# Sharing the float64-to-float32 conversion of the weights anew between VectorE, ScalarE and GpSimd, with a new written order of the opening and a later second half of batch 1's attention

## The chip, the cores and the metric

The kernel runs on one core of a Trainium2 chip. The metric is the device time of one execution in microseconds (us). The core has five engines with a queue of their own each: TensorE (PE, matrix products, with its weight loads PEld), VectorE (DVE), ScalarE (ACT), GpSimd (POOL) and SyncE (SP, which here only issues DMAs). Each takes its instructions in order.

## The reference, cut to what matters

Eight batches of 576 tokens with 8 heads of 64 attend to a memory of 32 slots per head, which is itself a weighted sum over the tokens. The result goes through a feed-forward layer with h * cos(h).

```
a    = softmax(phi over the 32 slots)                  # per token
k_m  = einsum(a, k);  v_m = einsum(a, v)               # 32 slots of 64 per head
attn = softmax(q @ k_m^T / 8)                          # over the 32 slots
x    = (attn @ v_m)  ->  4608 x 512
h    = x @ w_in                                        # 512 x 2048
out  = (h * cos(h)) @ w_out                            # 2048 x 512
```

`w_in` and `w_out` are float64 arrays (8 MB each); the others are float32.

## The kernel before, in words

**The fold.** x is never formed. Per batch, v_m is multiplied into w_in (the *fold*, `fold_psum`, L481), so h is a product of the attention weights (kept transposed in `aT`) and of the folded weights `vw`.

**Groups and steps.** The 4608 tokens are worked in twelve groups of 384. A step is one of 16 slices (128 wide) of the 2048 hidden columns of one group. It has a first product (`gemm1`, L548: into `hp`), h * cos(h) on ScalarE and VectorE (`act`, `act_end`), and a second product (`gemm2`, L600: into three accumulators), which runs four steps later (LAG). Group 0 uses float32 operands. The later groups use operands that are split into two float16 halves, three products for each. For this the weights must be scaled and split (`w_in_split`, L218; `w_out_split`, L209), with a scale that needs the largest sum of squares over all blocks of a weight (`m_of`, `s_of`).

**The opening.** Everything up to and with group 0's steps is written as single named steps, whose order is the string `ORDER` (L48). The instructions of a step go to the queues of their engines in that order, so an engine waits at the instruction whose turn it is. Names that matter here: `d_...` is a DMA issue on SP's queue (`d_kv0_c` the five pieces of batch 0's k and v, `d_q0_0` and `d_q0_1` its q, `d_in3` block 3 of w_in, `d_b1` batch 1's phi, k and v, `d_q1`, `d_q2` the later q); `warm*n` is n products of zeros; `ga` gathers the memory; `X`, `tpx`, `km`, `vm` turn it; `sc`, `tu`, `mx`, `sh`, `ex`, `to`, `no`, `ba`, `sp`, `sq` are scores, turn, maximum, shift, exp, total, normalise, turn back, high half and low half of the attention; `ffj` folds block j for batch 0 and `vfj` keeps the result; `g1_f` is gemm1 of group 0, `a1_f` to `a4_f` its activation (ScalarE, VectorE, ScalarE, VectorE), `g2_f` its gemm2; `fo1`, `hi0`, `hi1` fold and split for the loop; `m_`, `mt_`, `s_` are the scales.

**The conversion.** The chip has no float64 arithmetic, so each block of a weight (16 blocks of 1 MB, in0 to in7 and out0 to out7) is turned into float32 by bits (`conversion`, L154), over 1024 elements in each of 128 partitions:

- *scale*: the high word, taken as float32, times 2^-112, in place (GpSimd, L172)
- *low*: the top byte of the low word becomes the three lowest bits, as int16 (ScalarE for 13 blocks, L169; VectorE for 3, L171)
- *sign*: the top byte of the high word becomes the sign bit, as int16 (GpSimd for 13 blocks, VectorE for in0, in4 and out2; both L164)
- *join*: the scaled word shifted left by 3, or the two halves (VectorE, L176)
- *square*: the sum of squares of the block, for the scale (ScalarE, L179)

Three buffers take the loads in turn (in2 and in3 go to parts of `wo`), so a load waits for the join of the block that had its buffer before it.

**The loop.** Behind the opening, `for i in range(NF, 12 * NF)` (L983) writes steps 16 to 191; step 16 to 31 are group 1, which holds the last 192 tokens of batch 0 and the first 192 of batch 1. With them are written the splits of the weights (one of w_out and one of w_in in each step of group 1), the folds, and the memory and attention of later batches in small pieces. The order of the loop's instructions on each engine is set by a planner, which may also let them slip in between those of the opening's end.

Of the kernel before, what the change touches and what calls it, by code (L numbers as in the profile page):

```python
# [55 lines left out]
a2_4 square_out0 low_in4 vf3 a3_4 low_out1 max1 a1_5 g2_1 a4_4 square_in3 low_in6 g1_6 top1 join_in4 ff4 scale_out1
a1_6 d_b1 a2_5 a3_5 sign_in6 sign_out1 square_in4 d_in5 join_out1 a2_6 vf4 g1_7 a1_7 join_in6 a4_5 a3_6 d_out2 a2_7
g2_2 square_in1 blank1 a3_7 be1_0 be1_1 a4_6 a4_7 scale_in5 square_in6 low_in5 sign_in5 ex0_2 scale_out2 g1_8 d_out3
d_q1 to0_2 no0_2 g2_3 ba0_2 join_in5 x1_1 x1_0 g1_9 ga1_0 ga1_1 low_out2 sign_out2 join_out2 square_out1 ga1_2 a1_8
ga1_3 scale_out3 ff5 ga1_4 den1 X1_0 a1_9 a2_9 g2_4 sign_out3 low_out3 vf5 X1_1 sp0_2 a2_8 a3_9 d_in7 tpx1 scale_in7  # L60
# [1009 lines left out]
```

## Time and profile before

| | |
|---|---|
| median of 3 runs | 723.73 us (723.27 to 724.03) |
| the profiled execution | 723.56 us, of which the span of the profile is 721.8 |
| granted TensorE clock, mean | 0.99 |
| DMA moved | 66.17 MB |

The page gives one profiled execution. Its busy times are shares of the span. Its 40 slices show, per engine, in which part of the span it worked; one slice is 18 us. A row of a timeline is: start, duration, engine, source line, operation, what it writes and reads, shape and type, count and, in square brackets, the idle time before it with what ended it. A row of a group is the same without times: busy us, mean ns of one, and the idle time before them with its releasers. A row by stretch has: from and to, length, then busy us (and instructions) of PE, PEld, DVE, ACT and POOL, the granted clock, the DMA share and GB/s.

### The profile page before, as it was taken

How to read it: one execution, taken by the hardware profiler on the slowest of the kernel's cores; microseconds unless marked ns; L12 is line 12 of the kernel's file. 1: busy time of each engine (PE TensorE's matmuls, PEld its weight loads, DVE VectorE, ACT ScalarE, POOL GpSimd, SP SyncE). 2: the span in 40 equal slices, each digit the busy share in tenths (PEclk: the TensorE clock that was granted, in tenths of full speed). 3: DMA queues.
4: the chain of work that ended last, by engine and by line, in shares of the span. 5: the costliest groups of instructions: out<-in, count | busy, mean ns of one | idle time of the engine just before them, and what ended most of it. 6: DMA issues, size and time to landing. Idle time of an engine off the chain costs nothing.

```text
span 721.8 us, 11827 instructions
## 1 busy us (share of the span) xinstructions
PE 695.8 (96%) x4582; PEld 356.7 (49%) x4582; DVE 537.4 (74%) x1119; ACT 512.6 (71%) x946; POOL 89.8 (12%) x59
## 2 busy tenths in 40 slices
PE   7778988999999999999999999999999999999997
PEld 3334434555454444565444444565444444555553
DVE  3877989999897986579776886579776896576552
ACT  2658886899787686678767696678767786665652
POOL 0898880000000000000000100000000000000000
PEclk9989999999999999999999999999999999999999
DMA  8967792143625300152103220152100010100101
GB/s 299 341 250 264 249 321 59 51 106 75 199 67 165 111 1 1 45 165 67 45 1 111 72 94 1 45 166 66 45 2 1 1 45 1 45 1 1 45 0 45
DMA packets 31480, 66.17 MB, mean 92 GB/s; under 512 B 2176, under 2 KB 11456, under 8 KB 31424
## 3 DMA queue, kind: packets, MB, share of 16 engines
q1 hardware_dynamic: 27104, 57.55, 24.6%
q10 hardware_dynamic: 4320, 7.87, 2.8%
q8 instruction: 36, 0.59, 0.4%
q14 instruction: 20, 0.16, 0.1%
HBM read 51.77 MB, written 9.44 MB: 85 GB/s over the span
## 4 chain that ended last, share of the span: by engine, by line
PE 77%; DVE 7%; POOL 6%; DMA 4%; issue 3%; ACT 2%; SPq 1%; POOLq 0%; DVEq 0%; ACTq 0%
PE acc L613 43%; PE hp L562 23%; PE pv L492 3%; POOL wo L164 3%; PE acc L608 3%; PE psA L253 2%; DMA raw_in<-in_w_in 2%; POOL w_in_sb L164 2%; PE sc L395 1%; DMA phi<-in_phi 1%; POOL raw_out L172 1%; DVE u L583 1%; PE pv L486 1%; DVE wo L176 1%; DVE u L592 1%
## 5 line engine op out<-in xcount | busy, mean ns | idle before, releaser
L613 PE MATMUL acc<-wo,gp 128*128 128x512 f16 x1584 | 371.5, 379 | 0.0
L613 PEld LDWEIGHTS <-gp 128*128 128x128 f16 x1584 | 153.3, 98 | 161.5 <-issue 2.9
L562 PE MATMUL hp<-aT,vw 128*128 128x192 f16 (+1 forms) x1440 | 202.4, 284 | 0.5 <-DVE u L592 0.5
L562 PEld LDWEIGHTS <-vw 128*128 128x128 f16 x1440 | 125.3, 98 | 80.8 <-issue 28.3
L588 ACT ACTIVATE u<-u,quarter 128x384 f32<-128x384 f32 x176 | 107.0, 614 | 69.9 <-DVE u L583 69.3
L592 DVE SCALAR_TENSOR_TENSOR u<-hp,u 128x384 f32<-128x384 f32 x176 | 96.7, 554 | 63.1 <-ACT u L588 62.4
L583 DVE SCALAR_TENSOR_TENSOR u<-hp,cu,gp 128x192 f32<-128x192 f32 (+1 forms) x240 | 115.3, 504 | 27.8 <-ACT gp L578 26.5
L578 ACT ACTIVATE gp<-hp,cu 128x192 int32<-128x192 f32 (+1 forms) x240 | 110.7, 490 | 24.7 <-PE hp L562 17.3
L595 DVE TENSOR_TENSOR gp<-u,gp 128x384 f16<-128x384 f32 x176 | 96.4, 552 | 33.8 <-ACT gp L594 33.5
L594 ACT CAST gp<-u 128x384 f16<-128x384 f32 x176 | 88.2, 508 | 42.2 <-DVE u L592 41.7
L608 PE MATMUL acc<-wo,gp 128*128 128x512 f32 x96 | 48.0, 639 | 5.1 <-DVE wo L176 5.1
L333 POOL PARTITION_ALL_REDUCE l<-l x6 | 2.6, 441 | 305.2 <-DVE l L279 305.2
L501 DVE SCALAR_TENSOR_TENSOR vw<-pv,vw 128x512 f16<-128x512 f32 x48 | 33.0, 689 | 6.8 <-ACT vw L499 6.4
L499 ACT ACTIVATE vw<-pv 128x512 f16<-128x512 f32 x48 | 28.4, 592 | 7.7 <-PE pv L492 7.3
L608 PEld LDWEIGHTS acc<-wo,gp 128*128 128x128 f32 x96 | 18.9, 207 | 28.3 <-issue 20.0
L164 POOL TENSOR_SCALAR wo<-raw_out 128x1024 int16<-128x1024 int8 x7 | 30.9, 4420 | 0.5
L553 PE MATMUL hp<-aT,vf 128*128 128x384 f32 x64 | 26.9, 548 | 3.3 <-DVE gp L883 2.9
L629 ACT ACTIVATE ob<-acc,os 128x512 f32<-128x512 f32 x28 | 18.5, 684 | 15.3 <-PE acc L613 12.1
L253 PE MATMUL psA<-kv,phi 128*32 128x129 f32 (+3 forms) x640 | 23.3, 276 | 1.2 <-DMA kv<-in_kv_first 1.2
L588 ACT ACT_TABLE_LOAD x17 | 21.8, 1283 | 0.3
L253 PEld LDWEIGHTS psA<-kv,phi 128*32 128x32 f32 (+1 forms) x640 | 16.2, 109 | 11.4 <-issue 7.1
L395 PE MATMUL sc<-q,km 128*64 128x256 f32 (+3 forms) x192 | 19.9, 336 | 0.1
(159 smaller groups left out, 602.2 us busy)
## 6 DMA issues: line engine op xcount, KB each, us to landing
kv<-in_kv SPq DMA_DIRECT2D x28, 516.0 KB, 5.7
raw_out<-in_w_out SPq DMA_DIRECT2D x8, 1024.0 KB, 5.0
q<-in_qT SPq DMA_DIRECT2D x7, 1152.0 KB, 6.2
out<-ob ACTq DMA_DIRECT2D x30, 256.0 KB, 2.1
raw_in<-in_w_in SPq DMA_DIRECT2D x6, 1024.0 KB, 9.2
phi<-in_phi SPq DMA_DIRECT2D x7, 512.0 KB, 5.2
w_in_sb<-w_in_parts SPq DMA_DIRECT2D x12, 256.0 KB, 4.5
phiT<-in_phiT SPq DMA_DIRECT2D x4, 576.0 KB, 5.0
```

Of the source, the lines that this page charges most:

```text
L164: engine.tensor_scalar(out=halves[:, :, :, 1], in0=high_top, scalar1=0.0, scalar2=-32768.0, op0=ALU.is_lt, op1=ALU.mult)
L253: nc.tensor.matmul(psA[32 * j:32 * (j + 1), g * KV:g * KV + wide], lhsT=a[:n, c, h * M:(h + 1) * M], rhs=kvs[c][:n, h * wide:(h + 1) * wid ...
L501: nc.vector.scalar_tensor_tensor(out=vw[:, 1, g], in0=src, scalar=T, in1=vw[:, 0, g], op0=ALU.mult, op1=ALU.subtract)
L562: nc.tensor.matmul(hp[:, c0:c0 + n], lhsT=vw[:, wi, g, fo * P:(fo + 1) * P], rhs=aT[:, ai, g, c1:c1 + n], start=(k == 0), stop=(k == 5))
L578: ins = nc.scalar.activation(ni[:, c0:c0 + n], hp[:, c0:c0 + n], AF.Copy, scale=turns, bias=0.25)
L583: nc.vector.scalar_tensor_tensor(out=u[:, c0:c0 + n], in0=hp[:, c0:c0 + n], scalar=turns, in1=ni[:, c0:c0 + n], op0=ALU.mult, op1=ALU.subt ...
L588: nc.scalar.activation(u, u, AF.Sin, scale=TWO_PI_BELOW, bias=quarter)
L592: nc.vector.scalar_tensor_tensor(out=u, in0=hp[:, :GT], scalar=2.0 ** -17, in1=u, op0=ALU.mult, op1=ALU.mult)
L594: nc.scalar.copy(gp[:, 0], u)
L595: nc.vector.tensor_tensor(out=gp[:, 1], in0=u, in1=gp[:, 0], op=ALU.subtract)
L608: nc.tensor.matmul(accs[grp][t], lhsT=gp[:, t * P:(t + 1) * P], rhs=wo[:, f + 1], start=(f == 0), stop=(f == NF - 1))
L613: nc.tensor.matmul(accs[grp][t], lhsT=gp[:, gi, t * P:(t + 1) * P], rhs=parts[:, wi], start=(f == 0 and gi == 0 and wi == 0), stop=(f == N ...
```

## The change

- All sixteen sign passes are done by VectorE.
- The low passes: ScalarE keeps eight (in0, in2, in6, in7, out2, out3, out6, out7), GpSimd gets five (in3, in4, out1, out4, out5), VectorE has three (in1, in5, out0).
- The scaling of eight blocks (in1, in2, in3, in4, in6, in7, out0, out5) goes to ScalarE; GpSimd keeps eight.
- vm1's two copies go from VectorE to ScalarE.
- The written order of the opening is another, with 75 warm products in place of 50, and with d_in0 ahead of the kv loads and d_in1 ahead of d_q0_0.
- Batch 1's attention for tokens 256 to 575 (blocks 1 and 2 of its three) leaves the opening. It is written in pieces into steps 18 to 25 of the loop, and d_q2 with it. The maximum and scale of w_out (m_out, mt_out, s_out, os_0) move into step 17.
- The splits of w_out are written two steps later, those of w_in in every second step of groups 1 and 2 in place of every step of group 1.

```diff
-LOW_ACT = set('in0 in1 in2 in3 in6 in7 out1 out2 out3 out4 out5 out6 out7'.split())
-SIGN_DVE = set('in0 in4 out2'.split())
+LOW_ACT = set('in0 in2 in6 in7 out2 out3 out6 out7'.split())
+LOW_POOL = set('in3 in4 out1 out4 out5'.split())
+SCALE_ACT = set('in1 in2 in3 in4 in6 in7 out0 out5'.split())
+COPY_ACT = set('vm1'.split())
...
-d_phiT0 d_eye d_kv0_0 max0 d_kv0_1 d_kv0_2 e0_1 e0_0 blank0 warm*15 w0_0 d_kv0_3 w0_1 k0_0 warm*1 ga0_0 ga0_1 den0
-d_kv0_4 k0_1 d_q0_0 w0_2 d_in0 d_in1 k0_2 ga0_2 ga0_3 ga0_4 X0_0 scale_in0 X0_1 warm*4 tpx0 km0 att0 low_in0 vm0
-bound0 warm*3 sc0_0 tu0_0 sc0_1 tu0_1 mx0_0 sign_in0 sh0_0 ex0_0 join_in0 to0_0 no0_0 scale_in1 d_q0_1 ba0_1_0
-ba0_0_0 d_in2 square_in0 low_in1 warm*20 ff0 ba0_1_1 vf0 d_out0 ba0_0_1 d_in3 sc0_2 warm*7 g1_0 sign_in1 low_in2
...
+d_phiT0 max0 d_eye d_in0 e0_0 d_kv0_0 e0_1 d_kv0_1 warm*17 w0_0 d_kv0_2 scale_in0 w0_1 k0_1 d_kv0_3 k0_0 low_in0
+warm*5 ga0_0 d_kv0_4 sign_in0 w0_2 d_in1 warm*4 ga0_1 k0_2 join_in0 warm*5 ga0_2 den0 warm*5 ga0_3 warm*3 ga0_4
+square_in0 X0_0 blank0 d_q0_0 X0_1 warm*4 tpx0 d_in2 km0 d_q0_1 low_in1 d_in4 scale_in1 att0 warm*14 sc0_0 vm0
+sign_in1 sc0_1 join_in1 tu0_0 scale_in2 warm*1 ff0 tu0_1 mx0_0 sh0_0 d_out0 sign_in2 ex0_0 low_in2 to0_0 d_in3 vf0
+no0_0 warm*6 sc0_2 d_out1 ba0_0_0 scale_in4 low_in4 square_in1 ba0_1_0 blank1 ba0_0_1 ba0_1_1 warm*7 ff1 warm*4 g1_0
+sign_in4 tu0_2 vf1 g1_1 join_in4 ff4 a1_0 scale_out0 a2_0 g1_2 low_out0 a3_0 vf4 join_in2 sign_out0 scale_in3 a1_2
+a4_0 a1_1 ff2 g1_3 join_out0 a2_1 scale_out1 g2_0 vf2 a2_2 mx0_2 a3_1 a4_1 d_phiT1 d_in6 low_out1 square_in2 low_in3
+max1 bound0 g1_4 a1_3 g2_1 a2_3 square_in4 a3_2 d_b1 sign_in3 square_out0 low_in6 join_in3 sign_out1 a4_2 ff3
...
+            "low_POOL": lambda: low_bits(nc.gpsimd),
+            "scale_ACT": lambda: nc.scalar.mul(high.bitcast(F32), high.bitcast(F32), 2.0 ** -112),
+            "sign": lambda: nc.vector.tensor_scalar(out=halves[:, :, :, 1], in0=high_top, scalar1=0.0,
+                                                    scalar2=-32768.0, op0=ALU.is_lt, op1=ALU.mult),
...
+    def attend_rest():
+        for i in (1, 2):
+            do[1]["turn"](i, do[1]["scores"](i))
+            yield
+        load_q(2)
+        for what in ("top", "shift"):
+            do[1][what]((1, 2))
+        yield
+        do[1]["exp"]((1, 2))
+        do[1]["total"]((1, 2))
+        yield
+        do[1]["normalize"]((1, 2))
+        for i in (1, 2):
+            turned = do[1]["back"](i)
+            do[1]["high"](i, turned)
+            do[1]["low"](i, turned)
+            yield
+
+    REST = (18, 19, 20, 22, 24, 25)
...
-        if grp == 1:
-            w_out_split(f)
-        if NF <= i < 2 * NF:
-            w_in_split((i - NF) // 4, i % 4)
+        if i == NF + 1:
+            m_of(1, "out")
+            s_of("out", turn_column(st["m", "out"], "out"))
+            out_scales(0)
+        if NF + 2 <= i < 2 * NF + 2:
+            w_out_split(i - NF - 2)
+        if NF <= i < 3 * NF and i % 2 == 0:
+            w_in_split(*divmod((i - NF) // 2, 4))
...
+        if i in REST:
+            next(rest)
```

More of the change, by code (lines that the diff above doesn't have):

```diff
@@ L56 @@
[L56 to L60, printed above, removed]
@@ new lines @@
+a3_8 join_in7 scale_out3 ga1_4 g2_5 den1 sign_out3 scale_out4 low_out4 no0_2 X1_0 square_in7 a4_8 a3_9 X1_1 g1_10
+join_out3 acr0 d_out5 tpx1 square_in6 km1 ba0_2 g1_11 g2_6 bound1 a1_11 level0 a4_9 d_out6 a1_10 sign_out4 sp0_2
+acr1 m_in vm1 a2_10 join_out4 mt_in d_out7 s_in scale_out5 square_out2 a3_10 g1_12 level1 att1 a1_12 g2_7 sc_1 a4_10
+sc1_0 ff7 a2_11 scale_out6 a2_12 sc_0 low_out6 g1_13 tu1_0 fo1_0 a3_11 a3_12 low_out5 a4_12 mx1_0 hi0_0_0 vf7
+sign_out5 sh1_0 sq0_2 sign_out6 g2_8 square_out4 scale_out7 fo1_1 g2_9 a1_13 ex1_0 join_out5 d_b2 hi1_0_0 a4_11
@@ L162, in conversion, with low_bits @@
         high_top = flat.bitcast(I8).rearrange("p c (f t) -> p c f t", t=8)[:, :, :, 7]
-        def sign(engine):
-            engine.tensor_scalar(out=halves[:, :, :, 1], in0=high_top, scalar1=0.0, scalar2=-32768.0, op0=ALU.is_lt,
-                                 op1=ALU.mult)
+        def low_bits(engine):
+            engine.tensor_scalar(out=halves[:, :, :, 0], in0=low_top, scalar1=2.0 ** -5, scalar2=-31.0 / 64.0,
+                                 op0=ALU.mult, op1=ALU.add)
         spare = junk.rearrange("p (c f) -> p c f", c=dst.shape[1])
@@ L858, in step @@
             make[what]()
-        low = "ACT" if name in LOW_ACT else "DVE"
-        sign = "DVE" if name in SIGN_DVE else "POOL"
+        low = "ACT" if name in LOW_ACT else "POOL" if name in LOW_POOL else "DVE"
         put(f"low_{name}", lambda step=step, low=low: step("low_" + low))
-        put(f"scale_{name}", lambda step=step: step("scale"))
-        put(f"sign_{name}", lambda step=step, sign=sign: step("sign_" + sign))
+        scale = "ACT" if name in SCALE_ACT else "POOL"
+        put(f"scale_{name}", lambda step=step, scale=scale: step("scale_" + scale))
+        put(f"sign_{name}", lambda step=step: step("sign"))
         put(f"join_{name}", lambda step=step: step("join"))
@@ L947, in scaled @@
         split_half(b, st["vw", b, q], g, src, part)
-    for kind, name in enumerate(("in", "out")):
-        put(f"m_{name}", lambda kind=kind, name=name: m_of(kind, name))
-        put(f"mt_{name}", lambda name=name: turn_column(st["m", name], name))
-        put(f"s_{name}", lambda name=name: s_of(name))
+    put("m_in", lambda: m_of(0, "in"))
+    put("mt_in", lambda: turn_column(st["m", "in"], "in"))
+    put("s_in", lambda: s_of("in", r["mt_in"]))
     for b in range(2):
         put(f"sc_{b}", lambda b=b: scales(b))
-    put("os_0", lambda: out_scales(0))
     for g in range(2):
@@ L981, in attention_then_ffn @@
     gens = {}
+    rest = attend_rest()
     pending, begun = [(0, f, st["gp", f]) for f in range(NF - LAG, NF)], []
```

53 lines of the change are left out of this document (25 added, 28 removed).

## The prediction

> **What bounds the kernel now.** I read the page from the top, then busy times by stretch, the groups by form, and each engine's timeline.
>
> ```profile
> span 721.8 us, 11827 instructions
> PE 695.8 (96%) x4582; PEld 356.7 (49%) x4582; DVE 537.4 (74%) x1119; ACT 512.6 (71%) x946; POOL 89.8 (12%) x59
> PE   7778988999999999999999999999999999999997
> POOL 0898880000000000000000100000000000000000
> ```
>
> TensorE is full from slice 7 on; only the first seven slices (some 120 us) have holes, and in these alone GpSimd works. Whatever the change brings must come from there. The second view gives busy times by stretch (us in the stretch, then each engine's busy us and, in brackets, its instructions):
>
> ```profile
> 25.50:118.80 93.30, 76.74 (x313) 35.41 (x313) 77.24 (x134) 68.14 (x108) 73.55 (x31) 0.93 0.70 247
> 60.00:80.00 20.00, 17.78 (x129) 9.17 (x129) 17.73 (x29) 15.44 (x26) 17.60 (x7) 0.91 0.86 291
> 80.00:100.00 20.00, 19.52 (x76) 8.40 (x71) 19.34 (x42) 18.00 (x28) 16.80 (x9) 1.00 0.69 247
> 118.80:175.30 56.50, 56.50 (x352) 31.66 (x351) 53.74 (x109) 48.70 (x100) 0.31 (x1) 1.00 0.35 84
> 175.30:231.00 55.70, 55.70 (x439) 28.06 (x438) 45.54 (x102) 45.58 (x77) 1.00 (x3) 1.00 0.40 124
> ```
>
> 25.5 is the first g1 (f32 products of the opening), 118.8 the first f16 product of the loop, 175.3 the start of group 2. TensorE's holes lie before 118.8: 93.30 - 76.74 = 16.6 us behind the first g1. From 118.8 it never stops, so a microsecond saved before 118.8 is one off the end, unless the loop loses it again.
>
> TensorE's timeline gives the marks and the full-speed prices:
>
> ```profile
> 15.73 1.52 PE L395 MATMUL sc<-q,km 128*64 128x256 f32 x16
> 25.53 1.53 PE L553 MATMUL hp<-aT,vf 128*128 128x384 f32 x4 [0.36 <-DVE aT L426]
> 80.84 1.08 PE L518 MATMUL pvf<-w_in_sb,vm 128*64 128x256 f32 x8
> 94.28 1.45 PE L553 MATMUL hp<-aT,vf 128*128 128x384 f32 x4
> 113.10 0.29 PE L783 MATMUL across_out<-ident,m_out 128*128 128x128 f32 x1 [2.57 <-DVE m_out L937]
> 118.80 1.07 PE L562 MATMUL hp<-aT,vw 128*128 128x192 f16 x11
> 119.71 2.77 PE L608 MATMUL acc<-wo,gp 128*128 128x512 f32 x6
> ```
>
> The groups between 25.5 and 118.8 (count, busy us, mean ns):
>
> ```profile
> L608 PE MATMUL acc<-wo,gp 128*128 128x512 f32 x72 | 37.0, 653 | 5.1 <-DVE wo L176 5.1
> L164 POOL TENSOR_SCALAR wo<-raw_out 128x1024 int16<-128x1024 int8 x7 | 30.9, 4420 | 0.5
> L553 PE MATMUL hp<-aT,vf 128*128 128x384 f32 x64 | 26.9, 548 | 3.3 <-DVE gp L883 2.9 <-DVE aT L426 0.4
> L164 POOL TENSOR_SCALAR w_in_sb<-raw_in 128x1024 int16<-128x1024 int8 x4 | 17.0, 4252 | 0.2
> L176 DVE SCALAR_TENSOR_TENSOR wo<-raw_out,wo 128x1024 int32<-128x1024 int32 x8 | 13.1, 1643 | 8.7 <-POOL wo L164 8.6
> L172 POOL TENSOR_SCALAR raw_out<-raw_out 128x1024 f32<-128x1024 f32 x8 | 9.8, 1226 | 1.9 <-DMA raw_out<-in_w_out 1.8
> L164 POOL TENSOR_SCALAR w_in_sb<-wo 128x1024 int16<-128x1024 int8 x2 | 9.7, 4868 | 0.2
> L176 DVE SCALAR_TENSOR_TENSOR w_in_sb<-raw_in,w_in_sb 128x1024 int32<-128x1024 int32 x5 | 6.9, 1385 | 0.9 <-POOL w_in_sb L164 0.9
> L176 DVE SCALAR_TENSOR_TENSOR w_in_sb<-wo,w_in_sb 128x1024 int32<-128x1024 int32 x2 | 4.1, 2072 | 3.0 <-POOL w_in_sb L164 3.0
> ```
>
> Thirteen sign passes take 30.9 + 17.0 + 9.7 = 57.6 of GpSimd's 73.55 us, and VectorE's joins wait for them. That queue is the bound. TensorE's waste behind the first g1 is the 16.6 us of holes plus slowed products: twelve groups of six at 2.77 would be 33.2, not 37.0; sixteen g1 at 1.45 would be 23.2, not 26.9. Together **24 us**.
>
> **The change, part by part.** First the sign passes. VectorE's and GpSimd's timelines:
>
> ```profile
> 18.88 0.75 DVE L164 TENSOR_SCALAR w_in_sb<-raw_in 128x1024 int16<-128x1024 int8 x1
> 59.46 1.22 DVE L176 SCALAR_TENSOR_TENSOR w_in_sb<-raw_in,w_in_sb 128x1024 int32<-128x1024 int32 x1
> 70.38 4.34 POOL L164 TENSOR_SCALAR wo<-raw_out 128x1024 int16<-128x1024 int8 x1
> 71.02 1.89 DVE L176 SCALAR_TENSOR_TENSOR wo<-raw_out,wo 128x1024 int32<-128x1024 int32 x1
> ```
>
> Alone, VectorE signs in 0.75 and joins in 1.22; beside a GpSimd pass the join takes 1.89. Both ends of this price stay in the range.
>
> *VectorE's load* from the first g1 on, from 77.24: its fifteen joins took 13.1 + 6.9 + 4.1 = 24.1; fourteen remain behind g1_0, 17.1 alone (-7.0). Two signs there become thirteen:
>
> ```profile
> L164 DVE TENSOR_SCALAR wo<-raw_out 128x1024 int16<-128x1024 int8 x1 | 1.7, 1727 | 0.0
> L164 DVE TENSOR_SCALAR w_in_sb<-raw_in 128x1024 int16<-128x1024 int8 x1 | 1.1, 1083 | 0.0
> L171 DVE TENSOR_SCALAR w_in_sb<-raw_in 128x1024 int16<-128x1024 uint8 x2 | 2.1, 1063 | 0.0
> L412 DVE TENSOR_TENSOR at<-at,rm 128x640 f32<-128x640 f32 x1 | 0.8, 815 | 0.0
> L223 DVE SCALAR_TENSOR_TENSOR w_in_parts<-w_in_sb,s_in,w_in_parts 128x512 f16<-128x512 f32 x7 | 5.1, 746 | 0.5 <-ACT w_in_parts L222 0.5
> L412 DVE TENSOR_TENSOR at<-at,rm 128x512 f32<-128x512 f32 x1 | 1.6, 1552 | 0.0
> ```
>
> 13 x 0.75 - 2.8 = +7.0. Three low passes become two (-1.3, estimate). Batch 1's tokens from 256 on leave for the loop: four operations of 0.8 and eight smaller ones, some 6.7 by their shapes (-6.7). The seven w_in splits that had slipped in go back to the loop (-5.1); vm1, two short copies, goes to ScalarE (-0.6, estimate). Shift and normalise, stretched beside GpSimd (1.55 for 512 elements where 640 took 0.82), give back up to 3.5. That leaves 60. GpSimd keeps seven scalings at 1.23 and five low passes: about 31 us of work. 73.55 us of it had stretched VectorE by some 11 (joins 24.1 - 15 x 1.22 = 5.8, signs and low passes 1.9, shift and normalise 3.5), so 5 is put back: **65 us**.
>
> *Low pass on GpSimd*, not in the trace: at least 1.23 (its scaling, same count of elements), at most 8.8 (twice its sign pass); I take 4.42, since the sign row has the same widths and also two operations. Where it shows: low_in4, low_out1 and low_in3 follow one another on GpSimd. Walking the new order by hand from g1_0 with the durations of these rows (estimates), out1 is loaded and scaled at 36.4 and join_in3's turn on VectorE comes at 43.2. It gets its data at 36.4 + 2 x 4.42 = 45.2: **2 us** during which VectorE stands, with a2/a4 of the next steps behind it. At 1.23 this wait is gone; at 8.8 it is 11.
> The Trainium skill, GPSIMD Engine Reference, § 3.1, gives a plain one-input loop about 1.8 cycles an element at 1.2 GHz. By it 1024 elements would take about 1.5 us (estimate), and the sum below would be 2 us lower; the 4.42 us sign pass lies far off it.
>
> *Scaling on ScalarE*, not in the trace: between 1.04 (L916, exp over 1024 f32) and 1.36 (L169, strided bytes). Eight go there and five of thirteen low passes leave: +1.5 to +4 us for ScalarE, which is busy 68.14 of 93.30. That is hidden under TensorE and VectorE. If the cover were gone, it would be the 4.
>
> ```profile
> L916 ACT ACTIVATE phi<-phi 128x1024 f32<-128x1024 f32 x1 | 1.0, 1042 | 0.0
> L169 ACT ACTIVATE wo<-raw_out 128x1024 int16<-128x1024 uint8 x7 | 9.5, 1359 | 0.0
> ```
>
> *The written order.* d_in0 now stands ahead of the kv loads and d_in1 ahead of d_q0_0 on SP's queue. Loads land about in order of bytes:
>
> ```profile
> 13.09 0.64 PE L253 MATMUL psA<-kv,phi 64*32 64x128 f32 x16 [0.47 <-DMA kv<-in_kv_first]
> 21.42 1.26 POOL L172 TENSOR_SCALAR raw_in<-raw_in 128x1024 f32<-128x1024 f32 x1 [2.62 <-DMA raw_in<-in_w_in]
> ```
>
> (The first is TensorE's, the second GpSimd's timeline.) Before, in1 was the last of phiT, eye, kv, q0_0, in0, in1, and scaling it could start at 21.42. After, q0_0 is the last of exactly the same set, so sc0_0 starts at 21.4, not 15.73. From sc0_0 to g1_0 took 25.53 - 15.73 = 9.8, with sign_in0 (0.75) in VectorE's row; now about 8.9. **g1_0 at 30.3, +4.8** (28 to 32). The 75 warm products, 50 before, all stand ahead of g1_0, in time that TensorE waits anyway. The memory gather also waits longer: kv has 1 MB ahead of it that wasn't there.
>
> *Work moved out of TensorE's opening:*
>
> ```profile
> L395 PE MATMUL sc<-q,km 128*64 128x256 f32 x16 | 1.9, 385 | 0.0
> ```
>
> ff1 (L518 above) now runs ahead of g1_0 (1.0). Batch 1's later scores, half of this row and a 64-token rest, and m_out's transpose run in the loop (1.4): **-2.4**, of which **+1.4** comes back.
>
> *Waste behind g1_0.* TensorE's remaining work is 93.30 - 24 - 2.4 = 67, VectorE's 65: nearly balanced. While VectorE was busy 19.34 of 20, TensorE idled 0.48 (80 to 100); from 60 to 80, 2.22. Over 74 us that is 1.8 to 8.2; I take 4, plus the 2 us wait of join_in3, plus 2 for products slowed after holes (7.5 before, with 16.6 us of holes): **8 instead of 24, -16**.
>
> *The loop.* Batch 1's later tokens add 6.7 to VectorE in group 1, s_out's chain about 1; two w_out splits (0.75 each) and a splitting or so of w_in go to group 2: 53.74 + 7.7 - 2.5 = 59 against TensorE's 56.5 + 1.4 = 58. Cover is gone there, so what is late next is act's u and gp. ScalarE gains an exp (0.7) and one more pair of table loads in a stretch where it has 8 us free. Group 2 has 10 us free on VectorE and takes 8 w_in splits, 6. I cost it **+2**; if all of the added work showed, it would be 6.7, if backlog is absorbed by the four steps of lag, 0. The next load of q (d_q2) also moves into the loop; batch 2 first needs it near step 36. The order of the loop itself is a planner's, so what it hoists stays open.
>
> Sum: +4.8 - 2.4 - 16 + 1.4 + 2 = -10.2. The profiled execution took 723.56 (span 721.8), 0.17 under the median of 723.73. **723.56 - 10.2 = 713.4.**
>
> **The rivals.**
> - *A wait in place of the one removed (719.1).* Opening idles at the rate of 60 to 80 (8.2 + 2 + 2 = 12.2), and half of the added attention shows in the loop (3.4): 4.8 - 2.4 - 11.8 + 1.4 + 3.4 = -4.6. For it: every engine at 80% or more and queues in order, so one late load holds signs, and behind them a2 and a4. Against it: 80 to 100.
> - *TensorE runs on (706.2).* Idle 1.8 plus 1 slowed, loop 0: 4.8 - 2.4 - 21.2 + 1.4 = -17.4. For it: balanced loads; against: the join_in3 wait and the full group 1.
> - *Low passes on GpSimd hold VectorE's queue (724, slower).* At price p, join_in3 waits 36.4 + 2p - 43.2. At 8.8 that is 10.8 instead of 2 and join_out5 waits some 2 more: 713.4 + 8.8 + 2 = 724.2. It decides from p = 8.5 on. Against it: no GpSimd pass shown exceeds 4.87.
> - *GpSimd and VectorE exclude each other (729, slower).* If VectorE lost all 31 us of GpSimd's work and not 5, its 65 become 91 against the 75 planned from g1_0 on: +16. Against it: the join at 71.02 began and ended inside the pass of 70.38 to 74.72.
> The Trainium skill, SBUF — State Buffer, § SBUF: two separate sides, says that the shared port pair is an exclusive lock held for a whole instruction. By that rule this rival holds; the two rows above disagree, 0.67 us of stretch where it asks for a wait until 74.72.
> - *Late start and full loop cancel the gain (no change).* g1_0 at 32, waste 16 and loop 6.
>
> **How the numbers follow.** Forecast 0.54; wait in place 0.22; runs on 0.10; no change 0.04; low passes 0.07; exclusion 0.03. What can be told from no change is about 0.2% (1.4 us). So faster 0.86, same 0.04, slower 0.10. The range leaves out the slower cases, no change and half of "runs on", 0.19: 707 to 721. Waste of 2.8 to 12 and a loop cost of 0 to 6.7 lie in it.
>
> **What would show it.** Right: first g1 near 30, GpSimd busy near 35 us in the opening with low passes of 4 to 5 us, join without the POOL sign as releaser at 1.2 to 1.9, first f16 product of the loop near 105, TensorE full from there. Wrong: first g1 behind 33 (bytes do not set q0_0); TensorE holes in the loop's first 100 us above 5; ScalarE's scaling far above 1.4; VectorE idle behind GpSimd's low passes for more than 5 us in all.

## The result, and the profile after

| | before | after |
|---|---|---|
| median | 723.88 us (723.27 to 724.27, 4 runs) | 707.89 us (707.02 to 709.13, 4 runs) |
| the profiled execution | 723.56 us, span 721.8 | 707.53 us, span 705.4 |
| first scores / first g1 / first f16 product | 15.73 / 25.53 / 118.80 | 21.97 / 31.12 / 98.69 |

The ratio is 0.9781 (95% interval 0.9764 to 0.9798). The kernel became 16 us faster; 10.2 were forecast. The profiled executions differ by 16.03 us, their spans by 16.4. One of e6's four executions below (721.53 us) ran in a slower state of the chip and is left out.

The page of the changed kernel, the lines that answer to those of before:

```profile
span 705.4 us, 11869 instructions
PE 695.0 (99%) x4607; PEld 355.9 (50%) x4607; DVE 536.0 (76%) x1130; ACT 515.6 (73%) x953; POOL 31.2 (4%) x43
PE   8999999999999999999999999999999999999997
POOL 1122300000001000010000000000000000000000
```

TensorE's busy time is nearly the same (695.0 for 695.8), though it holds 25 more warm products: its holes over the whole span fell from 26.0 us to 10.4, and the first seven slices now show 8 and 9. GpSimd's 89.8 us became 31.2.

TensorE's timeline has the three marks:

```profile
21.97 1.52 PE L403 MATMUL sc<-q,km 128*64 128x256 f32 x16
31.12 2.85 PE L561 MATMUL hp<-aT,vf 128*128 128x384 f32 x8
98.69 1.15 PE L570 MATMUL hp<-aT,vw 128*128 128x192 f16 x12
```

Read from mark to mark: the first g1 comes 31.12 - 25.53 = 5.6 us later, the first f16 product 118.80 - 98.69 = 20.1 earlier, and the end 16.4 earlier. So the loop gave 3.7 back. The busy times by stretch of the changed kernel (the columns are those of before):

```profile
31.10:98.70 67.60, 67.51 (x290) 31.80 (x291) 62.97 (x120) 60.52 (x100) 16.82 (x12) 1.00 0.81 283
60.00:80.00 20.00, 20.00 (x109) 9.85 (x111) 17.61 (x49) 16.95 (x31) 6.12 (x5) 1.00 0.88 326
80.00:98.70 18.70, 18.70 (x59) 8.02 (x56) 17.76 (x31) 17.57 (x29) 1.48 (x2) 1.00 0.53 184
98.70:155.00 56.30, 56.24 (x361) 31.27 (x360) 55.08 (x119) 48.70 (x98) 0.62 (x2) 1.00 0.31 84
155.00:211.00 56.00, 54.66 (x412) 27.25 (x414) 51.58 (x109) 50.62 (x88) 1.00 (x3) 1.00 0.49 135
```

In the stretch from the first g1 to the first f16 product TensorE stands 67.60 - 67.51 = 0.09 us (16.6 before) at a granted clock of 1.00 (0.93 before), with VectorE busy 62.97 / 67.60 = 93% of it. Group 1 (98.7 to 155) has VectorE at 98%. The groups of the first of these stretches show what became of the products and of the conversion:

```profile
L616 PE MATMUL acc<-wo,gp 128*128 128x512 f32 x74 | 34.2, 599 | 0.0
L561 PE MATMUL hp<-aT,vf 128*128 128x384 f32 x64 | 23.9, 499 | 0.1
L181 DVE SCALAR_TENSOR_TENSOR wo<-raw_out,wo 128x1024 int32<-128x1024 int32 x8 | 10.2, 1281 | 0.1
L179 DVE TENSOR_SCALAR wo<-raw_out 128x1024 int16<-128x1024 int8 x8 | 6.7, 843 | 0.0
L166 POOL TENSOR_SCALAR wo<-raw_out 128x1024 int16<-128x1024 uint8 x3 | 4.9, 1636 | 0.2
L166 POOL TENSOR_SCALAR w_in_sb<-wo 128x1024 int16<-128x1024 uint8 x1 | 1.4, 1358 | 0.1
L175 ACT ACTIVATE raw_in<-raw_in 128x1024 f32<-128x1024 f32 x2 | 2.4, 1198 | 0.0
```

The acc products waited 5.1 us for joins before and wait for nothing now; VectorE's joins of w_out take 1281 ns in place of 1643, and the 8.6 us in which they waited for a GpSimd sign are gone. The low pass on GpSimd, which the trace of before doesn't show, takes 1.36 us, 2.21 in one case beside VectorE. The scaling on ScalarE takes 1.20, inside the 1.04 to 1.36 that bounded it.

### The profile page after: what moved, and what is told of

Its sections match the earlier page's. It is cut to its first block, busy times and chain, and to the rows that moved or that the text cites. A ratio compares the mean times of both kernels' runs of the same rounds, so it can differ in the third digit from the quotient of the medians.

```text
span 705.4 us, 11869 instructions
## 1 busy us (share of the span) xinstructions
PE 695.0 (99%) x4607; PEld 355.9 (50%) x4607; DVE 536.0 (76%) x1130; ACT 515.6 (73%) x953; POOL 31.2 (4%) x43
## 4 chain that ended last, share of the span: by engine, by line
PE 82%; DVE 7%; ACT 7%; DMA 3%; issue 1%; SPq 0%; DVEq 0%; ACTq 0%
PE acc L621 40%; PE hp L570 22%; PE acc L616 6%; PE pv L500 4%; PE hp L561 3%; PE psA L258 3%; PE sc L403 2%; DMA phi<-in_phi 2%; DVE u L591 1%; PE warm L659 1%; ACT gp L586 1%; DMA raw_in<-in_w_in 1%; ACT u L596 1%; DVE u L600 1%; PE pv L494 1%; PE pvf L526 1%
## 5 line engine op out<-in xcount | busy, mean ns | idle before, releaser
L570 PEld LDWEIGHTS <-vw 128*128 128x128 f16 x1440 | 124.9, 98 | 83.9 <-issue 29.1
L616 PE MATMUL acc<-wo,gp 128*128 128x512 f32 x96 | 44.4, 599 | 0.0
L561 PE MATMUL hp<-aT,vf 128*128 128x384 f32 x64 | 23.9, 499 | 0.1
L659 PE MATMUL warm<-zeros 128*128 128x512 f16 x75 | 19.6, 402 | 1.8 <-DVE zeros L654 1.8
```

Source lines behind the costliest of these rows:

```text
L561: nc.tensor.matmul(hp[:, :GT], lhsT=st["vf", q][:, g, fo * P:(fo + 1) * P], rhs=st["aTf"][:, g], start=(g == 0), stop=(g == 1))
L570: nc.tensor.matmul(hp[:, c0:c0 + n], lhsT=vw[:, wi, g, fo * P:(fo + 1) * P], rhs=aT[:, ai, g, c1:c1 + n], start=(k == 0), stop=(k == 5))
L616: nc.tensor.matmul(accs[grp][t], lhsT=gp[:, t * P:(t + 1) * P], rhs=wo[:, f + 1], start=(f == 0), stop=(f == NF - 1))
```

## The experiments

The marks shift with how soon k, v and q land, which differs between chips and executions, so the stretch from the first g1 to the first f16 product is compared beside the time. "Beside it" is the kernel before on the same chip; the 95% intervals are those of the ratio. All times in us.

| run | median | before beside it | ratio | first scores / g1 / f16 | g1 to f16 |
|---|---|---|---|---|---|
| e1 before, signs on VectorE | 719.68 | 722.42 | 0.9968 (0.9953 to 0.9983) | 19.18 / 29.11 / 113.91 | 84.80 |
| e2 before, sign as a minimum | 723.29 | 722.42 | 1.0009 (0.9995 to 1.0023) | 19.11 / 30.37 / 117.84 | 87.47 |
| e5 before, sign of an unsigned byte | 722.62 | 721.74 | 1.0010 (0.9993 to 1.0027) | 18.24 / 31.48 / 115.56 | 84.08 |
| e10 before, sign in four forms | 716.26 (one run) | 723.0 | | 18.38 / 30.29 / 111.12 | 80.83 |
| e9 after, again | 708.47 | 723.0 | 0.9801 (0.9777 to 0.9826) | 23.23 / 32.19 / 99.78 | 67.59 |
| e3 after, signs back on GpSimd | 726.12 | 722.42 | 1.0054 (1.0019 to 1.0088) | 22.16 / 35.53 / 114.66 | 79.13 |
| e4 after, old sharing of low and scale | 712.23 | 722.42 | 0.9871 (0.9839 to 0.9903) | 21.80 / 31.23 / 101.72 | 70.49 |
| e6 after, later tokens in the opening | 711.44 | 721.74 | 0.9855 (0.9829 to 0.9880) | 21.24 / 30.52 / 105.73 | 75.21 |
| e7 after, low pass three times | 714.98 | 721.74 | 0.9909 (0.9876 to 0.9942) | 24.87 / 33.81 / 106.02 | 72.21 |
| e8 after, q first | 706.65 | 721.74 | 0.9791 (0.9765 to 0.9816) | 21.02 / 32.20 / 100.86 | 68.66 |
| e11 after, q first, other passes later | 706.34 | 723.0 | 0.9775 (0.9754 to 0.9796) | 19.14 / 27.77 / 97.69 | 69.92 |
| e12 as e11, eight signs as products on GpSimd | 708.72 | 722.12 | 0.9810 (0.9791 to 0.9829) | 20.30 / 29.29 / 101.77 | 72.48 |

**The changed kernel again**

> The changed kernel itself, on the chip of these runs, so that the other runs can be set against it. By what it gave at first (707.89 us, 0.9781 of the kernel before) it should give 706 to 710 us and a ratio of 0.976 to 0.981. If the ratio were above 0.983, the 4 us that the earlier shares and the earlier place of the second batch's later tokens seemed to cost (712.23 and 711.75 us) would partly be a difference of chips.

708.47, as at first; the stretch is 67.59 (67.57 at first between the same marks), though it began 1.1 us later. So in the new order the stretch can be compared between executions, and 708.47 is what e3 to e12 are set against. In the old order it can't: e2 and e5, which change neither the work nor the time of before, have 87.47 and 84.08 where before has 93.27, mostly since their first g1 is 5 to 6 us later.

**The sign passes moved, alone (e1)**

```diff
-SIGN_DVE = set('in0 in4 out2'.split())
+SIGN_DVE = set('in0 out0 in1 out1 in2 out2 in3 out3 in4 out4 in5 out5 in6 out6 in7 out7'.split())
```

> The kernel before with one thing changed: all sixteen sign passes on VectorE, in the old order and with the old sharing. Theory (GpSimd's row of 57.6 us of sign passes is the bound): GpSimd keeps some 20 us of scaling, the first f16 product of the loop comes at 98 to 106 us instead of 118.8, time 704 to 712. Rival (the new written order carries the gain, since VectorE is full in the old one): at least 718.

Only 0.3% was gained, as the rival had it. The busy times by stretch and TensorE's waits in this run:

```profile
29.11:113.91 84.80, 73.98 (x312) 34.50 (x313) 80.10 (x145) 67.27 (x108) 17.50 (x17) 0.94 0.74 258
```

```profile
PE pvf L518 <- DVE w_in_sb L176: 6.1, 4, 3.4
PE hp L553 <- DVE gp L883: 3.8, 2, 3.4
```

GpSimd is down from 73.55 to 17.50 and no longer late with anything, but VectorE is now busy 80.10 of 84.80 (94%), and products wait for its joins and gp as before. Removing the bound brought the next one 0.3% further on. The move alone is not the 16 us.

**The signs moved back, in the changed kernel (e3)**

```diff
+SIGN_DVE = set('in0 in4 out2'.split())
...
-            "sign": lambda: nc.vector.tensor_scalar(
+            "sign_DVE": lambda: nc.vector.tensor_scalar(
...
+            "sign_POOL": lambda: nc.gpsimd.tensor_scalar(out=halves[:, :, :, 1], in0=high_top, scalar1=0.0,
+                                                         scalar2=-32768.0, op0=ALU.is_lt, op1=ALU.mult),
...
-        put(f"sign_{name}", lambda step=step: step("sign"))
+        sign = "DVE" if name in SIGN_DVE else "POOL"
+        put(f"sign_{name}", lambda step=step, sign=sign: step("sign_" + sign))
```

> The changed kernel with thirteen sign passes back on GpSimd as before (all but in0, in4, out2), everything else as changed. Theory: GpSimd's row is 57.6 + 5 x 1.36 + 8 x 1.2 = 74 us again and starts behind 26 us, the first f16 product of the loop comes at 112 to 122, time 718 to 730. Rival (the order carries the gain): 707 to 712.

17.7 us slower than the changed kernel and slower than the kernel before. Its groups in that stretch:

```profile
L184 DVE SCALAR_TENSOR_TENSOR wo<-raw_out,wo 128x1024 int32<-128x1024 int32 x8 | 13.8, 1736 | 8.3 <-POOL wo L182 8.2
L182 POOL TENSOR_SCALAR wo<-raw_out 128x1024 int16<-128x1024 int8 x7 | 30.0, 4291 | 6.2 <-ACT raw_out L176 5.9
```

The old picture is back: joins of 1736 ns that wait 8.2 us for GpSimd. So the whole gain hangs on GpSimd being rid of these passes in their form with a comparison (17.7 us in the new order; e12 below gives eight back in another form and keeps most of the gain), while in the old order their move brings 2 to 3. The gain is the two together: these passes off GpSimd, and an order and a load of VectorE that can use it. The order alone, the 25 more warm products, the later splits and the move of w_out's scale were not run by themselves.

**The sharing of low and scale (e4)**

```diff
-LOW_ACT = set('in0 in2 in6 in7 out2 out3 out6 out7'.split())
-LOW_POOL = set('in3 in4 out1 out4 out5'.split())
-SCALE_ACT = set('in1 in2 in3 in4 in6 in7 out0 out5'.split())
+LOW_ACT = set('in0 in1 in2 in3 in6 in7 out1 out2 out3 out4 out5 out6 out7'.split())
+LOW_POOL = set()
+SCALE_ACT = set()
```

> The changed kernel with the old sharing of the low passes (thirteen on ScalarE, none on GpSimd, three on VectorE) and all sixteen scalings on GpSimd; signs on VectorE and the new order stay. Theory (the signs are what matters): within 3 us of the changed kernel, 706 to 711, since ScalarE loses 8 x 1.17 and gains 5 x 1.36 us. Rival (the sharing of low and scale carries a good part): 712 or more.

3.8 us above e9 (5.1 by the ratios, whose intervals don't overlap); the stretch is 70.49, 2.9 longer, with 3.6 us of holes in TensorE. The rival was right: the sharing is worth some 4 to 5 us.

**The second batch's later tokens (e6)**

```diff
-    attend_in(1, (0,), ((0,),))
+    attend_in(1, (0, 1, 2), ((0,), (1, 2)))
...
-    attend_out(1, ((0,),))
+    attend_out(1, ((0,), (1, 2)))
...
-        if i in REST:
-            next(rest)
```

Their steps are written into the opening again, the scores, turns and shift in group 0's last steps and the rest behind them.

> The changed kernel with batch 1's tokens from 256 on written into the end of the opening again (scores, turns and exp around the first block's, the rest behind), d_q2 too; all else as changed. Theory (VectorE's 63 of 67.6 us in the opening leaves no room): VectorE gets 6.7 us more, TensorE 1.4, the first f16 product of the loop comes 3 to 7 us later than at 98.7, of which the loop returns what it no longer does: plus 1 to 5 us. Rival (the loop was as full as the opening, so it is the same work in another place): within 1 us of the changed kernel.

```profile
30.52:105.73 75.21, 71.20 (x309) 33.35 (x310) 69.17 (x128) 61.88 (x102) 16.19 (x13) 1.00 0.79 273
```

VectorE's work in the stretch is 69.17 for 62.97 (the prediction moved 6.7 out), TensorE's 71.20 for 67.51, and 4.0 us of holes open (0.1 in the changed kernel). The stretch is 7.6 longer, the time only 3.0 above e9 (3.9 by the ratios), within the theory: the loop does these operations for less than the opening, but not for nothing.

**The price of GpSimd's low pass (e7)**

```diff
-            "low_POOL": lambda: low_bits(nc.gpsimd),
+            "low_POOL": lambda: [low_bits(nc.gpsimd) for _ in range(3)],
```

> The changed kernel with each of GpSimd's five low passes done three times over (same result), so that a low pass costs about 4.1 us, which is the price the forecast took. If the forecast's waste of 8 us behind the first g1 hung on that price: join_in3 waits 1 to 2 us, VectorE's operations beside GpSimd stretch, plus 3 to 7 us. Rival (the order has slack for it, and the waste was overstated for other reasons): plus 0 to 2 us.

Busy times by stretch, then rows of GpSimd's timeline:

```profile
33.81:106.02 72.21, 68.92 (x293) 32.17 (x293) 67.10 (x119) 60.42 (x100) 31.57 (x23) 1.00 0.72 247
```

```profile
38.66 6.25 POOL L166 TENSOR_SCALAR wo<-raw_out 128x1024 int16<-128x1024 uint8 x3
45.00 4.23 POOL L166 TENSOR_SCALAR w_in_sb<-wo 128x1024 int16<-128x1024 uint8 x3
```

With a low pass of 4.2 us, about what the prediction took (4.42), the stretch is 72.21, 4.6 longer, TensorE has 3.3 us of holes in it, and VectorE's busy time rises by 4.1 though its work is the same. Most of that is sign passes on VectorE, 0.75 alone, which began beside such a pass and took up to 1.91. The time is 6.5 above e9; most of the rest goes with the later start of the profiled execution (g1 at 33.81 for 32.19). So 4 to 5 us hang on this pass, more than the 2 that the prediction put on it. But three products in a row hold VectorE back for all of their 4.2 us, and one pass with a comparison of that length doesn't, as the last section shows, so this isn't a clean price of a pass of 4.42.

**Why the sign pass on GpSimd is dear (e2, e5, e10)**

The first two left the pass on GpSimd and changed its form. e2 wrote it as a minimum with 0 times 32768, e5 as a comparison of the unsigned byte with 128.

```diff
-            "sign_POOL": lambda: sign(nc.gpsimd),
+            "sign_POOL": lambda: nc.gpsimd.tensor_scalar(out=halves[:, :, :, 1], in0=high_top, scalar1=0.0, scalar2=32768.0,
+                                                         op0=ALU.min, op1=ALU.mult),
```

> The kernel before with the sign pass left on GpSimd, but computed as min(x, 0) * 32768 instead of (x < 0) * -32768, same operands. In the changed kernel GpSimd's low pass (no comparison, same widths) took 1.36 us. If the comparison makes the 4.4 us, the pass falls to 1.2 to 1.6 us, GpSimd's work to about 38 us, and the time to 704 to 712. If it is the signed byte, 4.4 us and 723 to 724 stay.

```diff
-            "sign_POOL": lambda: sign(nc.gpsimd),
+            "sign_POOL": lambda: nc.gpsimd.tensor_scalar(out=halves[:, :, :, 1], in0=flat.bitcast(U8).rearrange("p c (f t) -> p c f t", t=8)[:, :, :, 7],
+                                                         scalar1=128.0, scalar2=-32768.0, op0=ALU.is_ge, op1=ALU.mult),
```

> The kernel before, sign passes where they were (thirteen on GpSimd), but GpSimd reads the top byte as an unsigned byte and compares with 128 (same value computed). The pass without comparison on a signed byte kept its 4.4 us, the low pass on an unsigned byte took 1.36: if the signed byte makes the price, the pass falls to 1.2 to 1.6 us. Then GpSimd has 38 us of work and VectorE none of the extra signs. Theory (without GpSimd's bound, VectorE's load in the opening is what holds the old order; with all signs on VectorE it gained 0.3% only): 709 to 716, clearly under the run with all signs on VectorE. Rival (the old written order itself holds it, whoever signs): 717 to 721. If the price stays, 723.

GpSimd's groups, of e2 and then of e5:

```profile
L174 POOL TENSOR_SCALAR wo<-raw_out 128x1024 int16<-128x1024 int8 x7 | 31.0, 4434 | 0.5
```

```profile
L174 POOL TENSOR_SCALAR wo<-raw_out 128x1024 int16<-128x1024 uint8 x7 | 30.5, 4357 | 0.5
```

Both stayed at 4.4 us and at the time of before. So neither `is_lt` itself nor the signed byte is the price. e5 also answers a rival that the prediction doesn't name, TensorE's clock. Busy times by stretch, of e2 and of e5:

```profile
30.37:117.84 87.47, 76.11 (x312) 35.22 (x313) 76.00 (x130) 67.58 (x108) 69.02 (x29) 0.92 0.70 246
31.48:115.56 84.08, 69.90 (x314) 32.60 (x313) 73.46 (x128) 66.69 (x107) 67.47 (x29) 1.00 0.70 248
```

The granted clock was 0.92 in e2, as in before (0.93), and 1.00 in e5's profiled execution, whose TensorE was busy 6.2 us less. That execution still took 720.07, 1.7 less than e2's, with 14.2 us of holes. So the slower clock of before is at most a small part of the 16 us.

e10 gave the thirteen passes four forms:

```diff
+        def sign_as(how):
+            src, s1, s2, op0, op1 = {
+                "A": (high_top, 0.0, 0.0, ALU.mult, ALU.add),
+                "B": (low_top, 0.0, -32768.0, ALU.is_lt, ALU.mult),
+                "C": (low_top, 2.0 ** -5, -31.0 / 64.0, ALU.mult, ALU.add),
+                "D": (high_top, 0.0, 0.0, ALU.mult, ALU.mult)}[how]
+            nc.gpsimd.tensor_scalar(out=halves[:, :, :, 1], in0=src, scalar1=s1, scalar2=s2, op0=op0, op1=op1)
```

> The kernel before, its 13 GpSimd sign passes in four forms that write the same place, the upper 16 bits of each weight: A, multiply and add on byte 7, signed (in1 to in3); B, compare and multiply on byte 3, unsigned (out0, out1, in6); C, the low bits' own operation on byte 3, unsigned (out3, out4, in5, in7); D, multiply and multiply on byte 7, signed (out5 to out7). The signs of these blocks are left out and some of their upper bits are others, so the output isn't the reference's; the number and width of the passes are those of before. Theory, the two operations set the price: A and C take about 1.4 us as the low pass of the changed kernel did (1.34 to 1.36), B and D about 4.4. Rival, the place written sets it: all four take 4.2 to 4.9 us. Third, the byte read sets it: B and C take 1.4, A and D 4.4. The time follows: 722 or so by the rival, a few us less by the others, since the stretch is bound by VectorE once GpSimd is freed (the run with all signs on VectorE gave 719.68).

GpSimd's timeline, one row of each form (in2 has A, out0 B, in7 C, out5 D), then the busy times by stretch:

```profile
27.35 1.38 POOL L174 TENSOR_SCALAR w_in_sb<-wo 128x1024 int16<-128x1024 int8 x1
30.42 4.02 POOL L174 TENSOR_SCALAR wo<-raw_out 128x1024 int16<-128x1024 uint8 x1
...
72.18 1.34 POOL L174 TENSOR_SCALAR w_in_sb<-raw_in 128x1024 int16<-128x1024 uint8 x1
...
95.31 1.34 POOL L174 TENSOR_SCALAR wo<-raw_out 128x1024 int16<-128x1024 int8 x1
```

```profile
30.29:111.12 80.83, 71.37 (x312) 33.32 (x313) 75.28 (x130) 66.93 (x108) 43.98 (x28) 0.98 0.75 265
```

The operation sets the price: B takes 4.02 to 4.53 in all three places, A, C and D 1.34 to 2.22 in all ten, at the same place written and from the same bytes. With multiplications and additions alone the pass takes a third of what it takes with a comparison or a minimum. The expectation had this for A and C and missed it for D. And the kernel before, in its old order and with its signs on GpSimd, comes to 716.26 in one run (before beside it: 720.98 to 724.07), 6.7 less: its queue of sign passes was the bound, as the prediction read it. That is more than e1's gain; VectorE gets no work here (75.28 us in the stretch for e1's 80.10).

**The late start (e8, e11)**

```diff
-warm*5 ga0_0 d_kv0_4 sign_in0 w0_2 d_in1 warm*4 ga0_1 k0_2 join_in0 warm*5 ga0_2 den0 warm*5 ga0_3 warm*3 ga0_4
-square_in0 X0_0 blank0 d_q0_0 X0_1 warm*4 tpx0 d_in2 km0 d_q0_1 low_in1 d_in4 scale_in1 att0 warm*14 sc0_0 vm0
-sign_in1 sc0_1 join_in1 tu0_0 scale_in2 warm*1 ff0 tu0_1 mx0_0 sh0_0 d_out0 sign_in2 ex0_0 low_in2 to0_0 d_in3 vf0
+warm*5 ga0_0 d_kv0_4 sign_in0 w0_2 d_q0_0 warm*4 ga0_1 k0_2 join_in0 warm*5 ga0_2 den0 warm*5 ga0_3 warm*3 ga0_4
+square_in0 X0_0 blank0 d_in1 X0_1 warm*4 tpx0 d_in2 km0 d_q0_1 d_in4 scale_in1 att0 warm*3 sc0_0 vm0
+sc0_1 tu0_0 warm*1 ff0 tu0_1 mx0_0 low_in1 sign_in1 sh0_0 scale_in2 join_in1 d_out0 sign_in2 ex0_0 low_in2 to0_0 d_in3 vf0
```

> The changed kernel with d_q0_0 issued ahead of d_in1 (as before the change), eleven warm products fewer, and in1's low, sign and join behind the first turns on VectorE. Theory of the late start (bytes ahead of q0_0 set the first scores): sc0_0 comes about 2.6 us earlier than at 21.97, the first g1 1.5 to 2.6 us earlier, and the time falls by as much as VectorE follows: minus 1 to 2.5 us. Rival (VectorE, busy 63 of 67.6 us, then is the bound): within 0.7 us.

By the ratios the time is within 0.1% of the changed kernel's: the rival. The first g1 did not come earlier (32.20), as low_in1 and sign_in1 stood ahead of sh0_0 on VectorE, and join_in1 behind it. e11 puts the first two behind sh0_0, and join_in1 with d_out1 further back:

```diff
-sc0_1 tu0_0 warm*1 ff0 tu0_1 mx0_0 low_in1 sign_in1 sh0_0 scale_in2 join_in1 d_out0 sign_in2 ex0_0 low_in2 to0_0 d_in3 vf0
-no0_0 warm*6 sc0_2 d_out1 ba0_0_0 scale_in4 low_in4 square_in1 ba0_1_0 blank1 ba0_0_1 ba0_1_1 warm*7 ff1 warm*4 g1_0
-sign_in4 tu0_2 vf1 g1_1 join_in4 ff4 a1_0 scale_out0 a2_0 g1_2 low_out0 a3_0 vf4 join_in2 sign_out0 scale_in3 a1_2
+sc0_1 tu0_0 warm*1 ff0 tu0_1 mx0_0 sh0_0 low_in1 d_out0 ex0_0 vf0 scale_in2 sign_in1 low_in2 to0_0 d_in3
+no0_0 warm*6 sc0_2 ba0_0_0 scale_in4 low_in4 ba0_1_0 blank1 ba0_0_1 ba0_1_1 join_in1 d_out1 warm*11 g1_0 ff1 a1_0 vf1
+sign_in2 square_in1 tu0_2 g1_1 sign_in4 a2_0 join_in4 scale_out0 g1_2 ff4 low_out0 a3_0 vf4 join_in2 sign_out0 scale_in3 a1_2
```

> The changed kernel with the first tokens' load ahead of the second block's, 11 warm-up products fewer, and, unlike the earlier run of this kind, the second block's low, sign and join passes put behind the shift of the scores (they were ahead of it and held the first GELU group up: 32.20 us instead of 31.12). Theory, the start of the first group is what is still to be had of the late start, since TensorE then runs on without holes: the first product of the group comes 1.2 to 2.2 us earlier (29 to 30 us), the first fp16 product 0.7 to 2 us earlier, time 705.5 to 707.5 and 1 to 2 us below the changed kernel's own run beside it. Rival, VectorE takes it back: its 62.9 us of work in the stretch from first group to first fp16 product become 65 or more, as the three passes fall into it, products wait for u or joins 1 us or more, and the time is within 0.7 us of the changed kernel's.

```profile
27.77:97.69 69.92, 68.63 (x299) 32.32 (x298) 64.89 (x122) 62.23 (x103) 17.31 (x15) 1.00 0.81 284
```

The first g1 is 4.4 us earlier than in e9, the first f16 product 2.1, the median 2.1 (the profiled executions differ by 3.4). Of the 4.4, 1.9 go with this execution, in which the memory was turned earlier (`tpx` at 17.99 for 19.88). Half of an earlier start is lost again in the stretch, where VectorE now has 64.89 us and TensorE stands 1.3. That lies between the theory and its rival. It is the fastest of all versions run, but its interval (0.9754 to 0.9796) overlaps that of the changed kernel beside it (0.9777 to 0.9826): it beats the kernel before, and beats the changed one probably, not surely.

**Cheap signs on GpSimd in e11 (e12)**

```diff
+SIGN_POOL = set('in2 in4 out0 in3 in6 out2 in5 in7'.split())
...
+            "sign_POOL": lambda: nc.gpsimd.tensor_scalar(out=dst.bitcast(BF16).rearrange("p c (f t) -> p c f t", t=2)[:, :, :, 1],
+                                                         in0=high_top, scalar1=2.0 ** -100, scalar2=2.0 ** -100,
+                                                         op0=ALU.mult, op1=ALU.mult),
```

> The kernel of the run before (first tokens' load ahead, 706.34 us) with eight sign passes of the stretch (in2 to in7 but not in1, out0 and out2) taken back to GpSimd as two multiplications, of the signed byte by 2^-100 twice into the upper half as bfloat16: the product underflows to plus or minus zero, whose upper 16 bits are the sign bit alone, so the computation is whole. Theory, GpSimd's price hangs on the operation: each pass takes 1.3 to 2.2 us, not the 4.2 to 4.9 of the comparison; VectorE sheds 8 x 0.75 = 6 us of its 64.9 in the stretch from first group to first fp16 product, the waits of products for joins (1.1 us) go, and the first fp16 product comes 0.5 to 2 us earlier than 97.69: 704.5 to 706.5 us. Rival, VectorE beside GpSimd's passes is drawn out by as much as it sheds (as its passes were in the kernel before), or TensorE, busy 68.6 of the 69.9 us, has nothing to gain: first fp16 product within 0.5 us of 97.69 and the time within 706 to 707.5. If the chip flushes the product to plus zero, the signs are lost and the output isn't the reference's; the times stand all the same.

The passes took 1.35 to 2.42, about as the theory had it, and yet nothing was gained: 708.72 for e11's 706.34 (the intervals of their ratios just overlap, so it is probably a loss, not surely), and a stretch of 72.48. VectorE's groups there show two reasons:

```profile
L185 DVE SCALAR_TENSOR_TENSOR w_in_sb<-raw_in,w_in_sb 128x1024 int32<-128x1024 int32 x5 | 7.6, 1518 | 3.0 <-POOL w_in_sb L180 3.0
L185 DVE SCALAR_TENSOR_TENSOR w_in_sb<-wo,w_in_sb 128x1024 int32<-128x1024 int32 x2 | 3.5, 1772 | 0.0
```

Joins wait 3.0 us for a sign on GpSimd, which has to queue there, and joins that could run are drawn out to 1.5 and 1.8 us. VectorE sheds 2.1 us of busy time, not 6, and gets 3.0 us of waiting. TensorE's waits for joins grow from 1.1 to 2.4 us:

```profile
PE pvf L530 <- DVE w_in_sb L185: 2.4, 2, 1.9
```

The rival's first half was right in the main (VectorE gives back some 4 of the 6 us). The first f16 product comes at 101.77, 4.1 later than e11's: 1.5 of that is a later first g1 in this execution, 2.6 the stretch.

## Why the prediction came out as it did

The direction and the range were right; the forecast was 5.5 us too high (713.4 for 707.89), and one term carries it. That the time lies in the range, by 0.9 us, is partly luck: it is nearer to the 706.2 of "TensorE runs on", which the range left out and which had 0.10, than to the forecast. Of the signs that the prediction named, the first g1 near 30 came true; GpSimd was busy 16.8 us in the opening, not 35, its low pass took 1.36 us, not 4 to 5, and the first f16 product came at 98.69, not near 105. The terms, with the marks above:

| term of the sum | forecast | measured |
|---|---|---|
| late start | +4.8 | +5.6 |
| work out of the opening | -2.4 | about -2.4 |
| waste behind the first g1 | 24 to 8, -16 | 24 to 0.7, -23.3 |
| work back in the loop | +1.4 | +1.35 |
| cover lost in the loop | +2 | +2.35 |
| sum | -10.2 | -16.4 |

The remaining work of 66.9 (93.30 - 24 - 2.4) and the measured stretch of 67.6 leave the 0.7. The second term is kept as forecast, and the busy time agrees: TensorE's fell by 9.2 in the stretch, of which 6.8 are products that are no longer slowed (7.5 before, 0.7 after).

**The bound** was read rightly (2.7 of the 57.6 us of sign passes lie ahead of the first g1, which changes nothing in it). e10 made ten of the thirteen sign passes cheap and left everything else: -6.7. e3 put them back in the new order: +17.7. What the prediction passed over is that the first move alone, without the rest, is worth 2 to 3 us, because VectorE fills up (e1).

**The late start** has the forecast size (first scores at 21.97 for 21.4, first g1 at 31.12 for 30.3), but not quite its cause. TensorE's timeline ahead of the scores, of before and then of after:

```profile
14.53 0.45 PE L778 MATMUL tpx<-ident,X 128*128 128x128 f32 x2
```

```profile
18.62 0.39 PE L787 MATMUL tpx<-ident,X 128*128 128x128 f32 x2
18.85 3.19 PE L659 MATMUL warm<-zeros 128*128 128x512 f16 x14
```

The turn of the memory (`tpx`), whose k and v now have in0 ahead of them, comes 4.1 us later, and fourteen warm products fill TensorE from there to the scores. q0_0 did land at about 21.5 (issued at 6.53, 15.0 to landing), as the bytes said, but the scores don't wait for it: in e3, e4, e6, e7 and e9 too they start 3.35 us behind `tpx`, in e7 2.1 us after q0_0 had landed. With q ahead of in1 and three warm products (e8, e11) they start 1.15 behind it. So the order of the loads and the warm products set the start together.

Nor does this term stand by itself. With the old order the executions of the experiments had their first g1 at 29.1 to 31.5, not 25.5, and the changed order 30.5 to 33.8 in e4, e6, e7 and e9; on the same chip the changed order's came between 1.0 us earlier and 2.3 later. And e2 and e5 took the time of before though their first g1 came 5 to 6 us later: GpSimd's queue sets the end there, and its scaling of in1 began at 21.4 to 21.9 in all three. The late start and the waste behind it share one sum; what counts is the first f16 product, forecast at 118.80 + 4.8 - 2.4 - 16 = 105.2 and measured at 98.69.

**The mis-sized term is the waste.** Of the 8 us, 4 were idle time of two nearly balanced engines, where TensorE stood 0.1; 2 were the wait of join_in3 behind GpSimd's low passes, where TensorE waited for no join; 2 were products slowed after holes, where 0.7 is left. VectorE's and GpSimd's timelines of the changed kernel:

```profile
44.25 1.22 DVE L181 SCALAR_TENSOR_TENSOR w_in_sb<-wo,w_in_sb 128x1024 int32<-128x1024 int32 x1 [0.51 <-DVE w_in_sb L179]
```

```profile
37.78 2.21 POOL L166 TENSOR_SCALAR wo<-raw_out 128x1024 int16<-128x1024 uint8 x1
40.07 1.36 POOL L166 TENSOR_SCALAR w_in_sb<-wo 128x1024 int16<-128x1024 uint8 x1
```

join_in3 waited 0.5 us, and the profile names its own sign, not GpSimd, whose low pass had ended at 41.43. The price of 4.42 came from the row of the sign pass. That was the wrong nearest row: e10 shows that the kind of operation decides, and that the scaling (1.23, two multiplications) was the right one. e7 shows that up to 4.6 us of the stretch hang on it, of the 7.3 by which the term was off. The idle share was taken from rows of before whose VectorE still waited for GpSimd; that this made it too high is argued, not shown.

The Trainium skill, GPSIMD Engine Reference, § 3.1, gives about 1.8 cycles an element as the best case of a tight loop; the estimate of about 1.5 us that the prediction worked out from it was nearer than the row chosen. The measured 1.36 is below it.

**VectorE's load** was forecast at 65 and is 62.97, against TensorE's 67 and 67.51. **ScalarE's scaling** was hidden as forecast: 1.20 each, and ScalarE busy 60.52 of 67.60.

**The loop** gave back 3.7 where 3.4 were forecast. Busy times by stretch, from the first f16 product to the end, of after and then of before:

```profile
98.70:705.40 606.70, 599.68 (x4112) 311.41 (x4110) 456.26 (x979) 440.56 (x833) 10.62 (x21) 1.00 0.20 61
```

```profile
118.80:721.80 603.00, 598.33 (x4097) 311.04 (x4095) 447.00 (x955) 434.21 (x822) 10.30 (x20) 1.00 0.19 58
```

TensorE has 1.35 us more work there and 2.35 more idle time (7.02 for 4.67). Its waits in the loop name where part of that is:

```profile
PE hp L570 <- DVE u L600: 1.5, 3, 0.7
PE sc L403 <- issue: 0.8, 1, 0.8
PE psA L258 <- ACT phi L312: 0.4, 1, 0.4
```

The first of these was 0.5 before, and u is what the prediction named as late next. The place is another than it said: in group 1 VectorE has 55.08 us of work, not 59, and TensorE stands 0.06; it stands 1.3 in the stretch behind (155 to 211), and the rest lies behind 300. So the size of this term was hit partly by luck.

**The rivals.** The sum of "a wait in place" gives 719.0, not 719.1. "TensorE runs on" (706.2) is what happened in the opening; the loop gave back more than it allowed. "A wait in place" is not there: no product waits for a join in the waits of the changed kernel. "Low passes hold the queue" needed 8.5 us a pass; three products of 4.2 us in all already cost e7 4 to 5 us, so its threshold was probably set too high. "GpSimd and VectorE exclude each other" was put aside on a row that doesn't carry it, as the last section shows; it cost little here, with GpSimd left with 16.8 us of work: the joins of the stretch took 18.2 us where fourteen at 1.22 would be 17.1.
